# A transformer block on one core: other load, evaluation and weight orders at both ends of the kernel

## The chip, the cores and the metric

The kernel runs on one core of one Trainium2 chip. The metric is the device time of one execution in microseconds, as the median of several runs. The core's engines are TensorE (PE, with its weight loads listed apart as PEld), VectorE (DVE), ScalarE (ACT), GpSimd (POOL) and SyncE (SP), which issues all DMAs of this kernel.

## The reference

A pre-norm block of multi-query attention, followed by a pre-norm gated feed-forward part. The sequence has 2048 tokens, the width D is 1024, there are 32 query heads of width 32 with one K and one V head, and F is 3584. All tensors are bf16.

```python
def layernorm(x):                      # no scale, no shift
    return (x - mean(x)) / sqrt(var(x) + 1e-5)

x  = A_x                               # [1, 2048, 1024]; B_x is not used
n  = layernorm(x)
q  = n @ wq                            # 32 heads of 32
k, v = n @ wk, n @ wv                  # one head of 32
p  = softmax(q k^T / sqrt(32))
h  = x + (p @ v, heads joined) @ wo
n2 = layernorm(h)
out = h + (sigmoid(n2 @ w_gate) * (n2 @ w_up)) @ w_down
```

## The kernel before, in words

**Tiles.** The tokens are 16 tiles of 128 (index t). A "half" hf is one token tile with 16 of its 32 heads, so there are 32 halves, and a "visit" is one half against one key tile kt: 512 visits. For each visit PE runs four S matmuls of 32 rows side by side (`emit_S`, L657), and ACT takes their 128 x 2048 scores through exp in two instructions of 1024 columns (L675) into a slot of bf16. There are 11 slots of their own (`Pr`) and 4 borrowed buffers (`QTb`, `hnT`, `hact`, `h_sb`) at the start. S lives in three pairs of PSUM banks, everything else that PE computes goes through two banks, `F_ps`.

**Stages of a half.** P V is done in parts of several key tiles (`mk_PV`, L737, `PARTS`, L691: 0 to 8 and 8 to 16), each part a group of matmuls with Vt; a slot comes free when its P V has run. The softmax sums are added up by DVE (`acc`, L650) and reduced by a small matmul group (`mk_SUM`). Half 0 (`RAW`) has its sums from a second set of P V groups with a matrix of ones. `finish` multiplies by the reciprocal sums into `OT`. The two halves of a token tile then give the output projection (`mk_OP`, L825), the second norm and the transposed `hnT` by DMA.

**Feed-forward.** Pass t (`mk_GU`, L927) has 7 groups of 512 columns of F. Gate and up are 8 matmuls each with `hnT` as the stationary and a weight slab as the moving operand (512 columns), so the result has tokens on the partitions. ACT makes tanh of the gate (L944), DVE joins it with up into `act_s` (L953), and a DMA transpose brings it to `hact` (L957). Down (`mk_D`, L977) is 4 groups of 28 matmuls of 256 columns with `wd_sb`. Slabs of gate and up stream in from memory for each pass (`load_next`, L888); the last two groups of a pass are kept for the next one, which runs in the opposite direction. w_down is loaded once (`load_wd`, L515), as the space of the first norms' tiles comes free, and a D group waits for all of it.

**Start.** x and the weights of Q, K, V are loaded in a written order (L293 to L315). The first norm's statistics are two DVE instructions per tile, an aggregate and two casts; the reciprocal root is made on POOL by an add and two powers (`stats`, L332, L357 to L363). Tiles 0 to 3 are transposed by PE (`mk_xT`), the later ones by DMA (`x_by_dma`, L391). K and V follow in `mk_KV`, Q for the first two tiles in `mk_Qc` (128 columns), for the others in `mk_Q`, which stores Q to memory to be read back by pairs of tiles. PSUM evictions go to ACT or DVE, whichever the planner has free first (`evac`, L263).

**What sets the order.** A planner in Python (`Plan`, L43) runs when the program is built. It holds estimated times for every instruction and a model of the DMA queue (`step`, L98; `LATE`, L45), picks for PE what to run next, and writes one fixed list per engine. On the chip each engine runs its list in order and waits on semaphores. PE's choices: an S as soon as its inputs are known and ACT has less than `run` of work queued; otherwise the group in hand, or the first ready class of `PRIOS` (L420), chosen by `qf`. `TUNE` (L19) holds the settings, and `few`, `pv_few`, `sum_few`, `hmin`, `h0`, `d_off` are thresholds in these choices.

Of the kernel before, what the change touches and what calls it, by code (L numbers as in the profile page):

```python
# [12 lines left out]
P = 128  # L13
# [5 lines left out]
TUNE = dict(pace0=280, rate0=300, swait=100, parts=2, raw=1, rl=0, nd=4, pc=16, rate=300, pace=250, xd=4, qf=2,  # L19
            dall=1, wo_late=1, nkn=1, few=0, rmin=600, hmin=3, h0=200, h1=350, hf=1.0, run=700, sum_few=0,  # L20
            pv_few=3, d_off=0, d_a=1, d_b=1, eb=0, eq=100)
# [19 lines left out]
class Plan:  # L41
# [3 lines left out]
    LATE = {"sl": 400.0, "rd": 300.0, "rb": 300.0, "hT": 400.0, "xt": 400.0, "ha": 400.0}  # L45
# [52 lines left out]
    def step(self, limit):  # L98
        best = None
        for e in self.ENG:  # L100
            h = self.heap[e]
            if h:
                s = min(self.start_of(o) for o in h)
                if best is None or s < best[0]:
                    best = (s, e)
        if best is None or (limit is not None and best[0] > limit):
            return False
        s, e = best
        h = self.heap[e]
        o = min((o for o in h if self.start_of(o) <= s + 1e-9), key=lambda o: (o.prio, o.seq))  # L110
        h.remove(o)
        if o.pace and self.pace_free > s:
            s2 = self.pace_free
            prev = [a for a in self.lists["act"][-6:] if a.end <= s2]
            if prev:
                o.deps.append(prev[-1])
            s = s2
        self.free[e] = s + o.occ
        o.start = s
        if o.nbytes:  # L120
            if o.pace:
                self.pace_free = s + o.nbytes / TUNE["pace0" if self.fast(s) else "pace"]
            go = max(s + 1500.0, self.dma_free)
            self.dma_free = go + o.nbytes / TUNE["rate0" if self.fast(s) else "rate"]
            o.end = self.dma_free + 750.0 + self.LATE.get(o.key.rstrip("0123456789_"), 0.0)
        else:
            o.end = s + o.lat
        o.pos = len(self.lists[e])
        self.lists[e].append(o)
        for u in o.users:  # L130
            u.ready = max(u.ready, o.end)
            u.missing -= 1
            if u.missing == 0:
                self.heap[u.eng].append(u)
        o.users = []
        return True
# [21 lines left out]
def bass_sequential_preLN__grouped_kv_mqa__glu_gated_glu__prompt_kernel(  # L158
# [31 lines left out]
    with ExitStack() as es:  # L190
# [113 lines left out]
        load_x(2)  # L304
        load_x(3)
        load_wq(0)
        for t in range(4, 6):
            load_x(t)
        load_wq(1)
        for t in range(6, 12):  # L310
            load_x(t)
        load_wq(2)
        for t in range(12, NT):
            load_x(t)
        load_wq(3)  # L315
# [16 lines left out]
        def stats(ph, tiles, srcs, deps, prio):  # L332
# [8 lines left out]
            for t, src, dp in zip(tiles, srcs, deps):  # L341
                s = n_st[0] % 8
                n_st[0] += 1
                a = pl.op("dve", lambda s=s, src=src: DVE.bn_stats(st[:, s, 0, :], src[:, 0:512]), dp, prio=prio,  # L344
                          occ=600, lat=756, order=[st_user.get(s)])
                b = pl.op("dve", lambda s=s, src=src: DVE.bn_stats(st[:, s, 1, :], src[:, 512:1024]), dp, prio=prio,  # L346
                          occ=600, lat=756, order=[st_user.get(s)])
                c = pl.op("dve", lambda s=s, t=t: DVE.bn_aggr(mv[:, ph, t, :], st[:, s, :, :]), [a, b], prio=prio - 1,
                          occ=110, lat=284)
                st_user[s] = c  # L350
                ag.append(c)
# [4 lines left out]
                      occ=90, lat=250)  # L356
            f = pl.op("pool", lambda: POOL.tensor_scalar(  # L357
# [11 lines left out]
        for tiles in ([0], [1], [2, 3], [4, 5], [6, 7], [8, 9], [10, 11], [12, 13], [14, 15]):  # L369
            r = stats(0, tiles, [x_sb(t) for t in tiles], [[x_ld[t]] for t in tiles], 3)  # L370
            for t in tiles:
                sv1[t] = r
        xnorm = {}
        xcent = {}
        for t in range(NT):
# [32 lines left out]
        make_norm1(0, [])  # L408
        make_norm1(1, [])
# [9 lines left out]
        head = ["xT", "KV", "Q0", "PV", "SUM", "OP", "hT"]  # L419
# [237 lines left out]
        def emit_S(v):  # L657
# [26 lines left out]
            if kt + 1 in PARTS:  # L684
                if kt == NT - 1 and hf not in RAW:
                    queues["SUM"].append(mk_SUM(hf))
                queues["PV"].append(mk_PV(hf, PARTS.index(kt + 1) - 1))
                if hf in RAW:
                    queues["PV"].append(mk_PV(hf, PARTS.index(kt + 1) - 1, True))

        PARTS = [(), (), (0, 8, 16), (0, 5, 10, 16), (0, 6, 11, 16), (0, 4, 8, 12, 16)][TUNE["parts"]]  # L691
# [6 lines left out]
        def in_row(few):  # L698
            return v_done[0] >= NV or pl.pe_mode == "row" or len(free_slots) <= few
# [22 lines left out]
        def finish(hf):  # L722

            if hf not in rb_ld or (hf, len(PARTS) - 2) not in oun_ev:
                return
# [6 lines left out]
                [oun_ev[(hf, len(PARTS) - 2)], op_last.get(c - 1)] + rb_ld[hf], prio=0, occ=600, lat=690)  # L732
# [4 lines left out]
        def mk_PV(hf, part, sums=False):  # L737

            kts = range(PARTS[part], PARTS[part + 1])
            final = part == len(PARTS) - 2  # L740

            def atoms(b):
                return [(mm(F_ps[DH * j:DH * (j + 1), b, :], ones[:, :] if sums else Vt[:, kt, :], slot_of[(hf, kt)][:, j * 512:(j + 1) * 512],
                            kt == kts[0], kt == kts[-1], tile_position=(0, DH * j)), 512, "col" if j == 3 else "col-", [],
# [30 lines left out]

            def first():
                return [exp_of[(hf, kt, i)] for kt in kts for i in range(2)] + [c_one if sums else v_ev.get(kt) for kt in kts]
# [149 lines left out]
        def mk_GU(t, i):  # L927

            gr = group_of(t, i)
            ho = hact[:, :].rearrange("p (a f b) -> p a f b", a=2, b=P)[:, t % 2, 4 * gr:4 * gr + 4, :]  # L930

            def atoms(w):
                def a(b):
                    us, ops = slab_at[(t, i, w)]
                    return [(mm(F_ps[:, b, :], hnT[:, dt, t % 2, :], us[dt // 4][:, dt % 4, :], dt == 0, dt == DT - 1),
                             512, "dense", [ops[dt // 2]] if dt % 2 == 0 else []) for dt in range(DT)]
# [12 lines left out]
            def after_u(b, last):  # L949
                k = n_act[0]  # L950
                n_act[0] += 1
                so = act_s[:, k % NST, :]
                e = pl.op("dve", lambda: DVE.scalar_tensor_tensor(  # L953
                    out=so, in0=tnh[:, :], scalar=1.0, in1=F_ps[:, b, :],
                    op0=ALU.add, op1=ALU.mult), [last, box["a"], act_dma.get(k - NST)], prio=0, **t_dve(512))
                box["e"] = e
                act_dma[k] = dma(lambda: SP.dma_start_transpose(ho, so), f"ha{t % 2}_{gr}", P * 1024, [e] + gu_deps(t),  # L957
                                 prio=0, occ=700.0)
                for f in range(4):
                    hact_ev[(t, 4 * gr + f)] = act_dma[k]  # L960
# [276 lines left out]
```

## Time and profile before

| | us |
|---|---|
| median of 4 runs | 1112.63 (1111.87 to 1114.09) |
| the profiled execution's own time | 1110.98 |
| its span, first to last instruction | 1109.2 |
| PE busy, share of the span | 1077.6 (97%) |
| ACT busy | 1009.4 (91%) |
| DVE busy | 836.2 (75%) |
| POOL busy | 65.7 (6%) |
| the 1008 exps into `Pr` (L675) | 945.1 |
| the 112 tanh (L944) | 70.5 |

In the profile a row of a group names the line, the engine, what is written and read, the shape and the count, then the busy time and the mean of one instruction. Nearly all matmuls have line 423, where the helper `mm` makes them, and are told apart by their operands: `S_ps<-QTb,kT` is S, `F_ps<-ring,hnT` or `F_ps<-Pr,hnT` is gate or up (with the slab in the ring or in former slots), `F_ps<-zone,hact` is down, `F_ps<-Pr,Vt` is P V, `F_ps<-wo_sb,OT` the output projection, `F_ps<-acc,sel` the sums, `F_ps<-zone` Q, K and V. In the rows by time, the first number is the start, the second the length of the merged stretch, and square brackets hold the idle time before it and the instruction that ended it. Matmuls overlap, so the busy time of PE does not say how much work it could still take; the distance from the start of one to the start of the next does.

### The profile page before, as it was taken

The numbers are of one execution on the slowest core, as the hardware profiler recorded it, in microseconds if no ns is written. First come the engines' busy times: TensorE is split into PE (matmuls) and PEld (weight loads), VectorE is DVE, ScalarE is ACT, GpSimd is POOL, SyncE is SP. The second block draws the span as 40 slices with busy tenths as digits, with TensorE's granted clock in tenths as the row PEclk, the third lists the DMA queues.
The fourth block names the chain that finished last, engine by engine and source line by source line (L and its number), as shares of the span: only waits on it lengthen the run. The fifth ranks groups of instructions, "written<-read, shape, count | busy, mean of one in ns | idle before, by whom it ended". The sixth has DMA issues, their size and how long they took to land.

```text
span 1109.2 us, 23778 instructions
## 1 busy us (share of the span) xinstructions
PE 1077.6 (97%) x9608; PEld 487.6 (44%) x9608; DVE 836.2 (75%) x1039; ACT 1009.4 (91%) x1160; POOL 65.7 (6%) x97
## 2 busy tenths in 40 slices
PE   5899997999999999999999999999999999999998
PEld 4533332444444444444444444444444444444456
DVE  8867978687777878787877878787877878787311
ACT  4899999999999999999999999999999999999010
POOL 4200100010010101010010101010010101010000
PEclk9999998999999999999999999999999999999999
DMA  9884499788959597887968597878958586988995
GB/s 262 177 264 145 108 297 261 208 225 195 268 152 239 158 256 176 226 217 200 254 161 239 150 265 177 225 217 174 282 159 239 160 242 167 232 216 196 277 294 135
DMA packets 305470, 235.56 MB, mean 212 GB/s; under 512 B 108496, under 2 KB 291792, under 8 KB 305360
## 3 DMA queue, kind: packets, MB, share of 16 engines
q1 hardware_dynamic: 305360, 234.03, 80.3%
q8 instruction: 76, 1.25, 0.5%
q14 instruction: 34, 0.28, 0.1%
HBM read 203.82 MB, written 8.12 MB: 191 GB/s over the span
## 4 chain that ended last, share of the span: by engine, by line
PE 70%; ACT 18%; DVE 6%; DMA 3%; issue 2%; SPq 1%; POOL 0%; POOLq 0%; DVEq 0%; ACTq 0%
PE F_ps L423 59%; ACT Pr L675 16%; PE S_ps L423 11%; DVE acc L650 2%; ACT tnh L944 1%; DVE st L344 1%; DVE st L346 1%; DMA rb<-r_scratch 1%; DMA ring<-in_B_w_gate_dram 1%; DMA hnT<-hn 0%; DMA Pr<-in_B_w_up_dram 0%; DMA ring<-in_B_w_up_dram 0%; DVE ring L393 0%; DVE ring L381 0%; DMA r_scratch<-r_sb 0%
## 5 line engine op out<-in xcount | busy, mean ns | idle before, releaser
L675 ACT ACTIVATE Pr<-S_ps 128x1024 bf16<-128x1024 f32 x1008 | 945.1, 1059 | 8.7 <-PE S_ps L423 8.4
L650 DVE TENSOR_TENSOR acc<-acc,Pr 128x2048 bf16<-128x2048 bf16 x430 | 525.1, 1221 | 79.0 <-ACT Pr L675 64.1
L423 PE MATMUL F_ps<-ring,hnT 128*128 128x512 bf16 x1672 | 413.4, 381 | 2.4 <-DMA ring<-in_B_w_up_dram 0.8
L423 PE MATMUL F_ps<-zone,hact 128*128 128x256 bf16 x1792 | 230.6, 275 | 1.0 <-DMA hact<-act_s 0.6
L423 PEld LDWEIGHTS F_ps<-ring,hnT 128*128 128x128 bf16 x1672 | 142.7, 97 | 191.2 <-issue 60.5
L423 PE MATMUL S_ps<-QTb,kT 32*128 32x512 bf16 x2048 | 202.8, 386 | 8.4 <-ACT Pr L675 7.1
L423 PEld LDWEIGHTS F_ps<-zone,hact 128*128 128x128 bf16 x1792 | 163.8, 98 | 68.1 <-issue 34.3
L423 PEld LDWEIGHTS S_ps<-QTb,kT 32*128 32x128 bf16 x2048 | 51.4, 91 | 193.1 <-ACT Pr L675 143.3
L423 PE MATMUL F_ps<-Pr,Vt 128*32 128x512 bf16 x2016 | 135.3, 382 | 0.9 <-ACT Pr L675 0.6
L944 ACT ACTIVATE tnh<-F_ps 128x512 f32<-128x512 f32 x112 | 70.5, 629 | 58.2 <-PE F_ps L423 58.2
L953 DVE SCALAR_TENSOR_TENSOR act_s<-tnh,F_ps 128x512 bf16<-128x512 f32 x112 | 76.6, 684 | 40.0 <-PE F_ps L423 38.2
L423 PE MATMUL F_ps<-zone 128*128 128x512 bf16 (+3 forms) x584 | 76.8, 279 | 2.7 <-DVE Vt L273 1.6
L423 PEld LDWEIGHTS F_ps<-Pr,Vt 128*32 128x32 bf16 x2016 | 43.9, 95 | 62.4 <-issue 27.2
L423 PE MATMUL F_ps<-wo_sb,OT 128*128 128x512 bf16 x256 | 64.0, 381 | 1.8 <-DVE OT L729 0.9
L357 POOL TENSOR_SCALAR zb<-mvb 128x1 bf16<-128x1 bf16 (+1 forms) x25 | 7.0, 282 | 977.4 <-DVE mvb L353 977.2
L770 DVE TENSOR_TENSOR oun<-F_ps,oun 128x512 f32<-128x512 f32 x32 | 22.1, 692 | 43.3 <-PE F_ps L423 43.3
L423 PEld LDWEIGHTS F_ps<-zone 128*128 128x128 bf16 x584 | 39.7, 99 | 31.8 <-issue 11.1
L990 DVE SCALAR_TENSOR_TENSOR h_sb<-F_ps,h_sb 128x256 bf16<-128x256 f32 x64 | 26.8, 419 | 33.6 <-PE F_ps L423 33.6
L712 DVE RECIPROCAL r_sb<-F_ps 128x64 f32<-128x64 f32 x31 | 17.3, 558 | 28.3 <-PE F_ps L423 28.2
L729 DVE TENSOR_TENSOR OT<-oun,rb 128x512 bf16<-128x512 f32 x32 | 22.0, 688 | 20.9 <-DMA rb<-r_scratch 20.9
L423 PEld LDWEIGHTS F_ps<-wo_sb,OT 128*128 128x128 bf16 x256 | 21.0, 97 | 35.7 <-issue 11.6
L650 DVE TENSOR_TENSOR acc<-Pr 128x2048 bf16<-128x2048 bf16 x31 | 36.0, 1163 | 0.0
(70 smaller groups left out, 319.5 us busy)
## 6 DMA issues: line engine op xcount, KB each, us to landing
ring<-in_B_w_gate_dram SPq DMA_DIRECT2D x308, 256.0 KB, 4.1
ring<-in_B_w_up_dram SPq DMA_DIRECT2D x304, 256.0 KB, 4.2
rb<-r_scratch SPq DMA_DIRECT2D x124, 64.0 KB, 2.9
zone<-in_B_w_down_dram SPq DMA_DIRECT2D x14, 512.0 KB, 5.0
Pr<-in_B_w_up_dram SPq DMA_DIRECT2D x24, 256.0 KB, 5.2
Pr<-in_B_w_gate_dram SPq DMA_DIRECT2D x20, 256.0 KB, 4.8
ring<-in_A_x_dram SPq DMA_DIRECT2D x16, 256.0 KB, 6.0
h_sb<-in_A_x_dram SPq DMA_DIRECT2D x16, 256.0 KB, 2.7
```

Source lines behind the costliest of these rows:

```text
L344: a = pl.op("dve", lambda s=s, src=src: DVE.bn_stats(st[:, s, 0, :], src[:, 0:512]), dp, prio=prio, occ=600, lat=756, order=[st_user.get(s)])
L346: b = pl.op("dve", lambda s=s, src=src: DVE.bn_stats(st[:, s, 1, :], src[:, 512:1024]), dp, prio=prio, occ=600, lat=756, order=[st_user.ge ...
L357: f = pl.op("pool", lambda: POOL.tensor_scalar(out=zb[:, ph, tk], in0=mvb[:, ph, tk, 1], scalar1=LN_EPS_BF16, scalar2=None, op0=ALU.add), ...
L423: return lambda: PE.matmul(o, lhsT=l, rhs=r, start=start, stop=stop, **kw)
L650: add_op[(hf, kt)] = pl.op("dve", lambda: DVE.tensor_tensor(out=a, in0=in0, in1=slot, op=ALU.add), dp, prio=6, **t_dve(2048, 1.92))
L675: exps[u] = pl.op("act", lambda i=i, pb=pb: ACT.activation(out=slot[:, i * 1024:(i + 1) * 1024].rearrange("p (a b) -> p a b", a=2), in_=S_ ...
L712: rc = pl.op("dve", lambda: DVE.reciprocal(r_sb[:, :], F_ps[:, b, 0:64]), [last, rd_ld.get(hf - 1)], prio=0, occ=64 * 8 / 0.96 + 20, lat=6 ...
L729: ot_ev[hf] = pl.op("dve", lambda: DVE.tensor_tensor(out=OT[:, 4 * hh:4 * hh + 4, :], in0=o.rearrange("p (a b) -> p a b", a=4), in1=r.rear ...
L770: oun_ev[(hf, part)] = pl.op("dve", lambda: DVE.tensor_tensor(out=o, in0=F_ps[:, b, :], in1=o, op=ALU.add), [last, oun_ev[(hf, part - 1)]] ...
L944: box["a"] = pl.op("act", lambda: ACT.activation(out=tnh[:, :], in_=F_ps[:, b, :], func=ACTF.Tanh, scale=0.5), [last, box.get("e")], prio= ...
L953: e = pl.op("dve", lambda: DVE.scalar_tensor_tensor(out=so, in0=tnh[:, :], scalar=1.0, in1=F_ps[:, b, :], op0=ALU.add, op1=ALU.mult), [las ...
L990: e = pl.op("dve", lambda: DVE.scalar_tensor_tensor(out=h_sb[:, t % NHB, sl], in0=F_ps[:, b, 0:DW], scalar=0.5, in1=h_sb[:, t % NHB, sl], ...
```

## The change

- The loads of wq's four quarters stand ahead of most x tiles: after x0, x1, wk and wv the order is x2, wq0, x3, wq1, x4, wq2, wq3, then the other x tiles.
- For tiles 0 and 1, the add and the reciprocal of the first norm run on DVE; only one power stays on POOL. The statistics of the first tiles are ordered after the centring of the tile before (`after`).
- P V parts of half 0 are key tiles 0 to 5, 5 to 10 and 10 to 16, those of half 1 are 0 to 6, 6 to 11 and 11 to 16. The later halves keep two parts.
- `qf` puts Q ahead of gate/up and down in PE's choice.
- In passes 0, 14 and 15 gate and up take the weight slab as the stationary and `hnT` as the moving operand: 32 matmuls of 128 columns in place of 8 of 512. The result has F on the partitions, so DVE writes `hact` itself, and there is no DMA transpose.
- The planner's DMA model and thresholds have other values, so the order of all lists shifts somewhat. In the lists, the order from the 97th S to the 480th has the same counts of each kind of work between S as before. After the last S there are 800 matmuls of 128 columns for gate and up (before: 184 of 512), 289 for down (288), and as before one P V part, one sum and 16 for the output projection. Ahead of the first S stand 8 transposes, 40 matmuls of 128 columns and 8 of 32 (before: 32, 48 with 7 of 256, and 16). The DMA transposes of `act_s` go from 112 to 91.

```diff
-TUNE = dict(pace0=280, rate0=300, swait=100, parts=2, raw=1, rl=0, nd=4, pc=16, rate=300, pace=250, xd=4, qf=2,
-            dall=1, wo_late=1, nkn=1, few=0, rmin=600, hmin=3, h0=200, h1=350, hf=1.0, run=700, sum_few=0,
-            pv_few=3, d_off=0, d_a=1, d_b=1, eb=0, eq=100)
+TUNE = dict(late=100, ws0=1, ws1=2, parts0=3, parts1=4, lord=2, h_ord=0, ho=0, ho2=3, pvl1=0, pvl2=0, col_ok=0,
+            pace0=310, swait=100, parts=2, raw=1, rl=0, nd=4, pc=16, rate=315, pace=310, xd=4, qf=1, dall=1,
+            wo_late=1, nkn=1, few=1, rmin=600, hmin=1, h0=0, h1=350, hf=1.0, run=700, sum_few=1, pv_few=4,
+            d_off=2, d_a=1, d_b=1, eb=0, eq=100)
...
-    LATE = {"sl": 400.0, "rd": 300.0, "rb": 300.0, "hT": 400.0, "xt": 400.0, "ha": 400.0}
+    LATE = {"sl": 465.0, "hT": -90.0, "xt": 100.0, "wd": -100.0, "xr": -300.0, "rb": -250.0, "ql": -500.0, "qs": -200.0,
+            "o": -500.0, "wo": 700.0, "x": -435.0}
+
+    SLOW = {"rb": 1.9, "ha": 2.5, "ql": 1.6, "wq": 1.1}
...
-        load_x(2)
-        load_x(3)
-        load_wq(0)
-        for t in range(4, 6):
-            load_x(t)
-        load_wq(1)
-        for t in range(6, 12):
-            load_x(t)
-        load_wq(2)
-        for t in range(12, NT):
-            load_x(t)
-        load_wq(3)
+        for c in ["xxqxxqxxxxxxqxxxxq", "qxqxxqxqxxxxxxxxxx", "xqxqxqqxxxxxxxxxxx", "xqxqxqxqxxxxxxxxxx", "xxqxqxqxqxxxxxxxxx"][TUNE["lord"]]:
+            if c == "x":
+                load_x(len(x_ld))
+            else:
+                load_wq(len(wq_ld))
...
+            if not ph and t0 < 2:
+
+                f = pl.op("dve", lambda: DVE.tensor_scalar(
+                    out=zb[:, ph, tk], in0=mvb[:, ph, tk, 1], scalar1=LN_EPS_BF16, scalar2=None, op0=ALU.add),
+                    [d], prio=prio - 1, occ=90, lat=250)
+                g = pl.op("pool", lambda: POOL.tensor_tensor(
+                    out=dsb[:, ph, tk], in0=zb[:, ph, tk], in1=half[:, 0:k], op=ALU.pow), [f, c0], prio=0,
+                    **slow(460 + 180 * k, 0))
+                h = pl.op("dve", lambda: DVE.reciprocal(rstd[:, ph, tk], dsb[:, ph, tk]), [g], prio=prio - 1, occ=90, lat=250)
+                return e, h
...
+            after = ((), ())
+            if tiles[0] in (1, 2):
+
+                p = tiles[0] - 1
+                after = (([sv1[p][0], xcent[p]], [xnorm[p]]), ([], [xnorm[p]]), ([xnorm[p]], ()), ([sv1[p][0], xcent[p]], ()))[TUNE["ho"] if p == 0 else TUNE["ho2"]]
...
+        def parts_of(hf):
+            return PARTS[TUNE["parts" if hf > 1 else "parts0" if hf == 0 else "parts1"]]
...
+            held_w = t < TUNE["ws0"] or t >= NT - TUNE["ws1"]
...
+                    if held_w:
+                        return [(mm(F_ps[:, b, k * P:(k + 1) * P], us[dt // 4][:, dt % 4, k * P:(k + 1) * P], hnT[:, dt, t % 2, :],
+                                    dt == 0, dt == DT - 1), P, "dense", [ops[dt // 2]] if k == 0 and dt % 2 == 0 else [])
+                                for k in range(4) for dt in range(DT)]
...
+                if held_w:
+                    e = pl.op("dve", lambda: DVE.scalar_tensor_tensor(
+                        out=ho, in0=tnh[:, :].rearrange("p (f b) -> p f b", b=P), scalar=1.0,
+                        in1=F_ps[:, b, :].rearrange("p (f b) -> p f b", b=P),
+                        op0=ALU.add, op1=ALU.mult), [last, box["a"]] + gu_deps(t), prio=0, **t_dve(512))
+                    done = e
```

## The prediction

> **What bounds the kernel now.** I read the page's slices first, to find where the engines are not full, then ScalarE's (ACT) and TensorE's (PE) instructions in order of time, then sums over chosen stretches. The slices:
>
> ```profile
> PE   5899997999999999999999999999999999999998
> ACT  4899999999999999999999999999999999999010
> PEclk9999998999999999999999999999999999999999
> ```
>
> One slice is 27.7 us. ACT is full from the third slice to the 37th and nearly empty in the last three; PE is short in slices 1, 2 and 7, and in the 7th its clock drops too. So there are three stages: a head, a long stretch in which ACT sets the pace, and a tail in which ACT has nothing and PE alone works. Sums by stretch (length, busy PE, PE weight load, DVE, ACT, POOL; clock; DMA share; GB/s):
>
> ```profile
> 50.00:90.00 40.00, 39.81 (x364) 15.55 (x362) 22.21 (x28) 35.50 (x40) 0.00 (x0) 1.00 0.76 245
> ...
> 185.00:198.00 13.00, 8.79 (x90) 4.51 (x86) 7.96 (x10) 10.89 (x13) 0.31 (x1) 0.74 0.50 131
> ...
> 380.00:1026.50 646.50, 646.50 (x5781) 285.69 (x5778) 514.98 (x591) 646.13 (x737) 30.37 (x30) 1.00 0.80 210
> 1026.50:1109.20 82.70, 76.22 (x539) 46.69 (x537) 19.16 (x34) 6.57 (x11) 1.35 (x3) 1.00 0.92 235
> ```
>
> From 380 to 1026.5 us ACT idles 0.4 us of 646.5: nothing that leaves its work alone can shorten this part. ACT's idle time sits in the head, and its exps are released by PE's S matmuls (square brackets: idle before, and who ended it):
>
> ```profile
> 19.25 2.85 ACT L675 ACTIVATE Pr<-S_ps 128x1024 bf16<-128x1024 f32 x3 [0.72 <-PE S_ps L423]
> ...
> 54.13 11.14 ACT L675 ACTIVATE Pr<-S_ps 128x1024 bf16<-128x1024 f32 x12 [2.28 <-PE S_ps L423]
> 84.07 0.60 ACT L272 ACTIVATE hact<-F_ps 128x512 bf16<-128x512 f32 x1 [0.42 <-PE F_ps L423]
> 86.47 4.69 ACT L675 ACTIVATE Pr<-S_ps 128x1024 bf16<-128x1024 f32 x5 [1.80 <-PE S_ps L423]
> ...
> 195.06 4.72 ACT L675 ACTIVATE Pr<-S_ps 128x1024 bf16<-128x1024 f32 x5 [2.11 <-PE S_ps L423]
> ```
>
> The first exp is at 19.25, the last ends at 1026.4. In between ACT is idle 9.5 us by the stretches (0.6 to 36 us, 0.7 to 50, 4.5 to 90, 0.2 to 140, 0.5 to 185, 2.1 to 198, 0.6 to 380, 0.4 after), so it works 997.7 us. **The ledger** is: first exp + ACT's work + its idle time, then the tail.
>
> PE in the tail, and one stretch of the head that prices a 128-column matmul:
>
> ```profile
> 25.16 2.51 PEld L423 LDWEIGHTS F_ps<-zone 128*128 128x128 bf16 x43 [0.23 <-issue]
> ...
> 1034.89 3.62 PE L423 MATMUL F_ps<-ring,hnT 128*128 128x512 bf16 x16
> 1038.34 1.67 PE L423 MATMUL F_ps<-Pr,hnT 128*128 128x512 bf16 x7
> ...
> 1060.87 3.22 PE L423 MATMUL F_ps<-zone,hact 128*128 128x256 bf16 x28
> 1063.93 2.75 PE L423 MATMUL F_ps<-Pr,hnT 128*128 128x512 bf16 x12
> ...
> 1096.71 9.78 PE L423 MATMUL F_ps<-zone,hact 128*128 128x256 bf16 x88 [0.59 <-DMA hact<-act_s]
> ```
>
> Start to start, a 512-column gate/up matmul takes 3.45/16 = 0.2156 us, a 256-column down matmul 3.06/28 = 0.1093, a 128-column one 2.51/43 = 0.0584. PE's last work before the last exps is an S at 1023.9; its tail runs from 1024.23 to 1106.49: 82.3 us. By the order of instructions it holds 184 gate/up (39.7 us), 288 down (31.5), 16 output-projection (3.45), one P V part (1.84) and one sum (0.42): 76.9. The other 5.4 are waits and drains: 3.7 are bracketed, 1.4 of these on DMAs (hnT 0.21, late slabs 0.33 and 0.28, the transposed hact 0.59). After PE come 2.7 us of output.
>
> **What the Trainium skill says.** "TensorE: Matmul & The Clock Gate", section "Back-to-back issue gap", gives N/2.4 + 2.5 ns for the isolated matmul (56 ns at N=128), but about 81 ns for a stream of weight load and matmul at N=128. The trace has 58.4 in such a stream, so I take 58.4; 56 and 81 are my bounds. The same page, "What's actually happening", says that PE's clock halves after about 3.4 us of little activity. The trace agrees: at 191.3 us, after waits, 14 down matmuls take 3.15 us (0.225 each, not 0.109). "GPSIMD Engine Reference", 3.1, has two software dispatch hops for each POOL instruction; here a 128x1 pow is 0.53 us (1.06 for two), a DVE cast of 128x2 0.17.
>
> **The change, part by part.**
>
> *First norms.* Tile 0 waited on POOL: behind four wk copies (to 6.36), then zb, pow and reciprocal pow, each interleaved with tile 1's; its normalisation started at 9.74 and the transposes at 10.27. After: add and reciprocal on DVE (no row for this size; 0.1 to 0.56, the 128x64 reciprocal; I take 0.17), one pow after only one wk copy. Worked through DVE's new order: statistics from 3.41, aggregate 4.7, zb ends 5.4, pow 5.45 to 6.0, reciprocal 6.3, then one x2 statistics half (0.6) that stands ahead of the normalisation and waits for x2 (issued 2.73, 3.8 us to land: 6.5). Normalise 7.1, transpose 7.65: 2.6 us earlier. The three wk copies now end near 7.1, before K needs them at 9.5.
>
> *Order to the first S.* Before, both tiles' transposes and K stood ahead of it; now 8 transposes, K, V and 32 Q matmuls of tile 0. From 7.65: 1.07 to the eviction, 0.69 on DVE (ACT took 1.02), K at 9.5, K/V to 10.75 at the cold clock, Q to 13.4 (half cold), 0.8 to S, 0.45 to exp: **first exp 14.7, 4.5 us earlier.** Second exp pair: tile 1's chain is now behind tile 0's on DVE: S at 17.75, exp 18.2, ACT idle 1.3. DVE carries four evictions (0.61) where it had two, and the kT ones; summing its new order puts tiles 2-3's kT at 24.3, the fifth S at 24.8 (28.09 before), ACT idle again 0.7. So 1.6 us of new idle time net of the old.
>
> *wq ahead of x.* wq1 follows 2.1 MB, not 2.6 (landed 12.7): near 11, needed at 12.2. On SP's queue x4 onward moves behind up to 1 MB, about 3 us at 350 GB/s; x5, due by 13.7 before, comes by 16 and DVE takes it at 18. Hidden by about 2 us; without that cover it costs what is late. The DMA transposes behind them wait for DVE anyway.
>
> *Small P V parts.* Idle at 54.13 and 86.47 is PE in a block of 32 + 32 P V matmuls that must free slots, after waiting for the eighth tile. Parts of 5 and 6 tiles start earlier. Between S 24 and 32 PE had 16.7 us of work (56 Q 12.1, P V 2.0, S 2.6) against ACT's 14.7 for 16 exps; the new order has at most 14.3 in any eight S. I take 4.3 of the 4.5 us as gone. Three more evictions, 2.1 us, lie on DVE, which is idle 17.8 of 40 us there.
>
> *Q ahead of gate/up, pass 0 held.* At 185 to 198 PE starved: pass 0's hidden tiles were transposed by DMA, and the last w_down loads (issued to 185.1, 5.0 us each) came at 190, so PE idled, cooled, and D ran at half rate: ACT's 2.11. Now Q ends by S 64, 9 of 14 w_down loads stand ahead of pass 0's later slabs (6 before), hact needs no DMA, and S 65 to 96 has 54.5 us of PE work against ACT's 62.3. That 7.8 us also covers pass 0's own excess: 448 x 0.0584 - 112 x 0.2156 = 2.0. I take 2.1 gone, and 0.9 of the small DMA-caused gaps from 140 to 380.
>
> *Ledger.* 14.7 + 997.3 (one tanh less, 0.48, ahead of the last exp) + idle 9.5 - 7.3 + 1.6 = 3.8: the last exp ends at 1015.8, **10.6 earlier.**
>
> *Tail, weights held in passes 14 and 15.* PE now has 800 matmuls of 128 columns after the last S, which is 200 of 512: 16 more than before, work that the shorter head left undone (it is not free: 3.4 us), and the dearer form (2.8 more). 46.7 + 289 x 0.1093 + 3.45 + 1.84 + 0.42 = 84.0. Waits 5.4 - 1.4 = 4.0, as no transposed hact is waited for, and 10 transposes leave the saturated DMA (1.1 share, 288 GB/s from 1040 to 1090) while 2 MB more slabs come: about even, with PE slower. Tail 88.0, **5.7 longer.** At 56 or 81 ns it is 3.8 or 23.8 longer. Next in the way is PE's own work.
>
> *Sum.* -10.6 + 5.7 = -4.9. The profiled execution took 1110.98 us (span 1109.2), 0.15% below the median of the runs, 1112.63; I apply the difference to the median: **1107.7 us.**
>
> **Rivals.**
>
> *A, more comes back.* The tail's waits mostly go (2.3 more) and DVE's lag costs nothing (2.0): 1103.4. For: the tail's largest wait, 0.93 on OT, has filler. Against: P V and the sum still end one chain.
>
> *B, the idle time only moves.* PE's order is fixed: a D group that meets a late w_down load holds all S behind it, or the x2 wait on DVE delays tile 0. If only 2.4 of the 7.3 us go, -5.7 + 5.7 = 0: 1112.6. For: five w_down loads still stand at the end of pass 0. Against: PE has work ahead of them.
>
> *C, slower.* Held-weight matmuls run at the skill's streaming 81 ns, as each must load its own weights: 800 x 0.0226 = 18.1 more in the tail: 1125.8. It decides from 0.0584 + 4.9/800 = 64.5 ns. Against: 43 in a row at 58.4.
>
> That the change does not take place is excluded by the order of instructions.
>
> **How the numbers follow.** Forecast 0.56, A 0.20, B 0.13, C 0.11. Measurement tells about 0.2% from no change: below 1110.4 is faster, above 1114.9 slower. Forecast, A and a little of B: faster 0.79; the rest of B and an edge of the others: same 0.11; C and B's worst: slower 0.10. C and half of B are left out of the range, 1101.5 to 1112.8.
>
> **What would show it.** Right: first exp near 14.7; no ACT gap over 1 us from 50 to 200; clock whole there; last exp near 1016; tail near 88; 128-column gate/up matmuls 58 ns apart. Wrong: long ACT idle at the second or fifth S; D stalled near S 90; over 64 ns per held matmul; slab waits in the tail.

## The result, and the profile after

The changed kernel takes 1109.43 us, the median of 34 runs (1106.85 to 1113.43); the kernel before takes 1112.64 beside it (53 runs, 1110.27 to 1115.61). The ratio is 0.9971, 95% interval 0.9965 to 0.9976: 3.2 us faster, where the forecast was 4.9. The profiled execution took 1110.42 (span 1108.6), 1.0 above its median, and that of before 1110.98 (span 1109.2), 1.7 below its own. So the two traces differ by only 0.6 us, and what follows reads stages, not spans.

The slices of the changed kernel (27.7 us each):

```profile
PE   6899999999999999999999999999999999999999
ACT  4999999999999999999999999999999999998010
PEclk9999999999999999999999999999999999999999
```

PE's seventh slice is full now (9, before 7), ACT's second too (9, before 8), and the clock is whole, where it had an 8 in the seventh slice. Sums by stretch (length, busy PE, PE weight load, DVE, ACT, POOL; clock; DMA share; GB/s), the last two cut at the new end of the exps:

```profile
50.00:90.00 40.00, 39.08 (x402) 15.26 (x403) 31.83 (x43) 39.69 (x45) 1.47 (x2) 1.00 0.85 269
185.00:198.00 13.00, 11.67 (x107) 5.39 (x104) 11.53 (x13) 13.00 (x16) 0.00 (x0) 1.00 0.60 189
380.00:1023.50 643.50, 639.82 (x5814) 285.67 (x5811) 509.00 (x582) 639.40 (x727) 30.35 (x30) 1.00 0.79 207
1023.50:1108.60 85.10, 80.71 (x1146) 73.65 (x1143) 19.98 (x35) 7.24 (x13) 1.34 (x3) 1.00 0.75 232
```

ACT's idle in 50 to 90 us fell from 4.50 to 0.31, and in 185 to 198 from 2.11 to nothing. But from 380 us on ACT idles 4.1 us, where it had idled 0.4. ACT in order of time shows where (some of its longer pieces of idle time, in square brackets):

```profile
15.54 1.94 ACT L690 ACTIVATE Pr<-S_ps 128x1024 bf16<-128x1024 f32 x2 [0.59 <-PE S_ps L438]
...
312.31 1.94 ACT L690 ACTIVATE Pr<-S_ps 128x1024 bf16<-128x1024 f32 x2 [0.92 <-PE S_ps L438]
...
565.35 1.94 ACT L690 ACTIVATE Pr<-S_ps 128x1024 bf16<-128x1024 f32 x2 [0.92 <-PE S_ps L438]
...
691.54 1.94 ACT L690 ACTIVATE Pr<-S_ps 128x1024 bf16<-128x1024 f32 x2 [0.83 <-PE S_ps L438]
...
1003.94 4.71 ACT L690 ACTIVATE Pr<-S_ps 128x1024 bf16<-128x1024 f32 x5 [1.01 <-PE S_ps L438]
```

Each of the late ones is an S that PE issued late, and PE's own waits name what held it. Who waited for whom, PE and its weight load, 198 to 1005 us (total us, times, longest); in the kernel before no DMA is in this list:

```profile
PE F_ps L438 <- DMA ring<-in_B_w_up_dram: 4.9, 10, 1.0
...
PEld F_ps L438 <- DMA ring<-in_B_w_up_dram: 13.6, 20, 1.4
```

So slabs of the up weights arrive late. PE in the tail:

```profile
1032.13 3.74 PE L438 MATMUL F_ps<-hnT,ring 128*128 128x128 bf16 x64
1035.70 1.11 PE L438 MATMUL F_ps<-hnT,Pr 128*128 128x128 bf16 x17
1038.10 1.89 PE L438 MATMUL F_ps<-wo_sb,OT 128*128 128x512 bf16 x8 [1.29 <-DVE OT L748]
...
1093.56 12.39 PE L438 MATMUL F_ps<-zone,hact 128*128 128x256 bf16 x112
```

64 matmuls of 128 columns take 3.57 us from start to start (1032.13 to 1035.70), 55.8 ns each, each with a stationary of its own. The only long wait is 1.29 on OT, and nothing waits for a DMA.

To set runs side by side I added the gaps between ACT's instructions in order of time, from one numbered exp to another (of 1024; two make a visit), and took the time from the end of PE's last S to its last matmul as the tail. All in us; the ratio is to the kernel before on the same chip, and the last column is the median time from the first issue of the seventh group's up slab to its first use (the weight load of the group's first up matmul), passes 2 to 12; a dash is a time that was not read. Single runs apart, the kernel before had medians between 1111.25 and 1112.64 beside these, so the ratio decides, and ratio x 1112.6 puts a run on the scale of the expectations.

| kernel | ratio (95%) | first exp | idle to exp 65 | 65 to 185 | 185 to 1024 | last exp ends | tail | issue to use |
|---|---|---|---|---|---|---|---|---|
| before | 1 | 19.25 | 5.8 | 2.8 | 0.9 | 1026.4 | 82.2 | 15.2 |
| changed | 0.9971 (0.9965-0.9976) | 15.54 | 3.4 | 0 | 6.5 | 1023.6 | 84.4 | 4.6 |
| pace 250 | 0.9975 (0.9965-0.9985) | 15.12 | 3.1 | 0 | 5.5 | 1022.1 | 85.8 | 5.1 |
| tail of 512 columns | 1.0003 (0.9992-1.0015) | 15.23 | 2.9 | 0 | 3.9 | 1020.3 | 87.5 | 4.4 |
| x first | 1.0019 (1.0008-1.0030) | 16.07 | 4.6 | 0.8 | 7.3 | 1027.8 | 83.7 | 4.5 |
| two P V parts | 1.0050 (1.0032-1.0069) | 15.48 | 8.9 | 0.7 | 7.1 | 1031.7 | 86.4 | 6.1 |
| resident weights | 0.9933 (0.9919-0.9947) | 15.55 | 3.2 | 0 | 3.4 | 1019.1 | 84.7 | - |
| D one group later | 1.0009 (0.9998-1.0020) | 15.41 | 2.9 | 0 | 7.2 | 1022.8 | 85.9 | 6.4 |
| GpSimd reciprocals | 1.0099 (1.0077-1.0120) | 16.43 | 1.1 | 0.7 | 6.9 | 1020.1 | 104.4 | - |
| Q late | single run | 15.42 | 2.9 | 0.6 | 7.2 | 1020.2 | 110.6 | - |
| store late | 0.9950 (0.9938-0.9962) | 15.53 | 3.2 | 0 | 2.9 | 1018.9 | 83.3 | 5.3 |
| hnT late | 0.9959 (0.9946-0.9972) | 14.85 | 3.0 | 0 | 3.2 | 1019.1 | 83.7 | 6.5 |
| both late | 0.9960 (0.9948-0.9973) | 14.91 | 3.2 | 0 | 3.4 | 1018.9 | 83.4 | 7.0 |
| no order of norms | single run | 17.73 | 1.0 | 0 | 9.2 | 1022.8 | 103.5 | - |

### The profile page after: what moved, and what is told of

Its sections match the earlier page's. It is cut to its first block, busy times and chain, and to the rows that moved or that the text cites. A ratio compares the mean times of both kernels' runs of the same rounds, so it can differ in the third digit from the quotient of the medians.

```text
span 1108.6 us, 25728 instructions
## 1 busy us (share of the span) xinstructions
PE 1079.3 (97%) x10616; PEld 531.6 (48%) x10616; DVE 842.7 (76%) x1051; ACT 1007.5 (91%) x1155; POOL 65.2 (6%) x93
## 3 DMA queue, kind: packets, MB, share of 16 engines
q8 instruction: 84, 1.38, 0.5%
HBM read 203.82 MB, written 8.12 MB: 191 GB/s over the span
## 4 chain that ended last, share of the span: by engine, by line
PE 57%; ACT 31%; DMA 5%; DVE 4%; issue 2%; SPq 1%; POOL 0%; DVEq 0%
PE F_ps L438 48%; ACT Pr L690 29%; PE S_ps L438 9%; DMA ring<-in_B_w_up_dram 2%; ACT tnh L972 2%; DVE acc L665 1%; DMA r_scratch<-r_sb 1%; DMA rb<-r_scratch 0%; DMA zone<-ring 0%; DMA ring<-in_A_x_dram 0%; DVE st L342 0%; DVE ring L398 0%; DVE st L344 0%; DVE ring L386 0%; SPq L929 0%
## 5 line engine op out<-in xcount | busy, mean ns | idle before, releaser
L665 DVE TENSOR_TENSOR acc<-acc,Pr 128x2048 bf16<-128x2048 bf16 x429 | 523.9, 1221 | 78.1 <-ACT Pr L690 62.3
L438 PE MATMUL F_ps<-ring,hnT 128*128 128x512 bf16 x1456 | 361.8, 381 | 5.2 <-DMA ring<-in_B_w_up_dram 4.9
L438 PEld LDWEIGHTS F_ps<-ring,hnT 128*128 128x128 bf16 x1456 | 123.2, 97 | 172.4 <-issue 53.3
L438 PEld LDWEIGHTS F_ps<-zone,hact 128*128 128x128 bf16 x1792 | 163.1, 98 | 63.4 <-issue 32.7
L988 DVE SCALAR_TENSOR_TENSOR act_s<-tnh,F_ps 128x512 bf16<-128x512 f32 x91 | 62.2, 684 | 23.5 <-PE F_ps L438 21.3
L438 PE MATMUL F_ps<-hnT,ring 128*128 128x128 bf16 x912 | 61.0, 219 | 1.4 <-DMA ring<-in_B_w_gate_dram 1.0
L438 PEld LDWEIGHTS F_ps<-hnT,ring 128*128 128x128 bf16 x912 | 52.4, 98 | 9.9 <-issue 7.6
L438 PEld LDWEIGHTS F_ps<-zone 128*128 128x128 bf16 x584 | 40.5, 100 | 34.2 <-issue 11.1
```

The lines of the kernel that those rows point to most:

```text
L438: return lambda: PE.matmul(o, lhsT=l, rhs=r, start=start, stop=stop, **kw)
L665: add_op[(hf, kt)] = pl.op("dve", lambda: DVE.tensor_tensor(out=a, in0=in0, in1=slot, op=ALU.add), dp, prio=6, **t_dve(2048, 1.92))
L988: e = pl.op("dve", lambda: DVE.scalar_tensor_tensor(out=so, in0=tnh[:, :], scalar=1.0, in1=F_ps[:, b, :], op0=ALU.add, op1=ALU.mult), [las ...
```

## The experiments

**First round: is it the pace of the transfers, and what is each part worth?** My first theory was that SyncE's list and its pacing make slabs late; its rival, that PE's own order does.

Pace 250: `TUNE: pace=310` becomes `pace=250`.

> The changed kernel with the pace of its transfers at 250 bytes per ns, as the kernel before had it, instead of 310: TensorE's order stays the same but for one spot of three matmuls in the tail, only the order and the spacing of SyncE's issues in the middle differ. Theory 1 (the 7.6 us of the lead that are lost between 198 and 1022 us go to gate/up slabs that land late, because SyncE's list puts stores and transposes ahead of them): the waits of PE for ring<-in_B_w_up_dram (18.5 us of idle in front of PE's F_ps groups in the middle) change clearly with the list. If this pace restores the old spacing, ACT's idle in 198:1000 falls from 5.5 to 1-2 us, the last exp ends 3 to 5 us earlier and the time is 1104.5 to 1106.5. Theory 2 (the loss comes from PE's own order, as D matmuls or P V parts that stand ahead of a score): nothing moves, 1109.4 +- 0.6, ACT's idle in the middle 5 to 6 us. A time above 1111 would say that the list matters but that 310 is the better pace of the two.

Measured: ratio 0.9975, ACT's idle in the middle 5.5 us, slab waits of 3.4 (PE) and 12.8 (weight load) in place of 4.9 and 13.6. The pace is not the cause; the waits survive another spacing.

Tail of 512 columns: `ws1=2` becomes `ws1=0`.

> The changed kernel with the weights-held form of gate/up only in pass 0, so the last two passes stream 512 columns again (200 matmuls of 512 in the tail for 800 of 128, one D matmul fewer) and their products go through a DMA transpose. All up to the last exp is as in the changed kernel. Theory 1: the held form costs 800 x 0.0557 = 44.6 us in the tail and the other 200 x 0.2156 = 43.1, so 1.5 us of work are saved here, and PE waits again for the transposed products, 1 to 4 us as in the tail of the kernel before: 1109 to 1112, the tail 84 to 87 us, last exp unchanged. Rival (the held form saves the tail nothing, its waits were hidden by D matmuls): 1107.5 to 1108.5, tail near 83.

Measured: ratio 1.0003, 0.32% above the changed kernel's, 3.6 us; tail 87.5. PE in that tail, where products go through a DMA transpose again:

```profile
1060.36 0.61 PE L438 MATMUL F_ps<-zone,hact 128*128 128x256 bf16 x4 [3.04 <-DMA hact<-act_s]
...
1095.85 9.78 PE L438 MATMUL F_ps<-zone,hact 128*128 128x256 bf16 x88 [0.64 <-DMA hact<-act_s]
```

Two waits of 3.7 us in all for transposed products: the held form costs 1.5 us of work and saves these. The expectation's first theory holds in its mechanism; the time (1.0003 x 1112.6 is 1113.0) and the tail lie somewhat above its ranges. This run has the changed kernel's lists up to its last passes, yet lost 3.9 us in the middle where the changed kernel's profiled execution lost 6.5. So what late slabs cost differs between executions with the same lists, and one profiled execution does not tell it to better than some 2.6 us.

x first: `lord=2` becomes `lord=0`, the old order of loads.

> The changed kernel with the old order of loads (wq's quarters after x tiles 3, 5, 11 and 15), all else as changed; TensorE's order of the tail and SyncE's list of the middle are the same. Theory 1 (Q's weights bind the first exp once the norms are short): first exp 2 to 3 us later than 15.5, near 18, and the lead that is lost is carried to the end of the first half or further: 1110 to 1112. Rival (the first dozen exps are bound by the norms and the later tiles, so that by exp 21 the order of loads no longer shows): first exp later by as much, but the time 1109.4 +- 0.7, because at exp 21 both are alike.

Measured: 1.0019, 0.48% or 5.3 us worse than the changed kernel, of which 2.5 are there by exp 185 (199.28 against 196.78). The first exp moved by only 0.5, not by 2 to 3. The fifth moved, from 20.75 to 25.69: ACT waits 2.31 and 1.38 us for PE's Q and K between them. So the order of loads pays, but not where I expected it, and both statements on the first exp were wrong.

Two P V parts: `parts0=3, parts1=4` become `2, 2`.

> The changed kernel with the old P V parts (0, 8, 16) in halves 0 and 1 too. Theory 1 (the small parts take away the gaps of ACT at about 54 and 84 to 86 us): one or both gaps come back within 50 to 95 us, 2 to 4.5 us of ACT idle there against 0.3, and the time is 1111.5 to 1114. Rival (the gaps went with the earlier Q, or the lead gained there is lost again to late slabs in the middle whatever its size): the gaps come back or not, but the time stays within 1108.5 to 1110.5.

Measured: 1.0050. ACT in order of time shows that both gaps are back:

```profile
53.31 3.77 ACT L690 ACTIVATE Pr<-S_ps 128x1024 bf16<-128x1024 f32 x4 [1.80 <-PE S_ps L438]
58.32 7.44 ACT L690 ACTIVATE Pr<-S_ps 128x1024 bf16<-128x1024 f32 x8 [1.24 <-PE S_ps L438]
87.07 0.60 ACT L277 ACTIVATE hact<-F_ps 128x512 bf16<-128x512 f32 x1 [2.98 <-PE F_ps L438]
```

The idle time to exp 65 is 8.9, 5.5 more. The theory on the small parts holds; the rest of the loss (8.8 us in all) lies behind, in an order that the planner has changed as well, with one stop of 2.88 us at 621.

**Second round: which slab, and why.** Set against the times of the groups, PE's waits for slabs fall in the seventh, the last group of a pass. In pass 8 the seven groups start, from the first one's start, at 0, 4.3, 15.4, 26.5, 35.1, 51.3 and 57.9 us before, and the next pass at 62.3; after, at 0, 11.1, 22.2, 30.8, 46.9, 53.5 and 58.0, and the next at 63.4. It is the same sequence of gaps, turned by one group. (Counts of work between the S are the same as before, as said with the change; they do not show which group falls where.) Before, the close pair behind the seventh was the first and second group, and their slabs are resident. After, it is the sixth and seventh, and the seventh needs new slabs, in slots that come free when the fifth is done. What SyncE does at that point of the changed kernel, in order of time (start, length of issue):

```profile
675.06 0.36 SPq L1032 DMA_DIRECT2D out_dram<-h_sb  x1
676.51 1.12 SPq L929 DMA_DIRECT2D ring<-in_B_w_gate_dram  x2
678.06 0.35 SPq L844 DMA_DIRECT2D h_sb<-in_A_x_dram  x1
678.46 0.94 SPq L929 DMA_DIRECT2D ring<-in_B_w_gate_dram  x2
679.45 2.57 SPq L875 DMA_TRANSPOSE hnT<-hn  x1
682.06 1.26 SPq L991 DMA_TRANSPOSE hact<-act_s  x1
683.37 1.61 SPq L929 DMA_DIRECT2D ring<-in_B_w_up_dram  x3
685.09 0.48 SPq L733 DMA_DIRECT2D r_scratch<-r_sb  x1
685.61 0.59 SPq L929 DMA_DIRECT2D ring<-in_B_w_up_dram  x1
```

SyncE issued nothing from 668.5 to 675.06: it stood at the store, which waits for the pass's last D (DVE adds that one to `h_sb` at 674.62, for 0.42 us). Over the middle these stores are the second largest of SyncE's waits (total us, times, longest; the row names the DVE cast that ends next to that addition):

```profile
SPq L929 <- PE F_ps L438: 148.4, 55, 6.7
SPq L1032 <- DVE mvr L353: 83.8, 13, 6.8
```

The row of the kernel before:

```profile
SPq L997 <- DVE mvr L355: 48.7, 13, 4.0
```

The fifth group's last matmul starts at 677.8, so its slot is free shortly after; the up slab is issued from 683.37 to 685.61, behind a store, a load and two transposes, and PE, which comes to the group's up matmuls at 687.4 (first weight load), waits in front of the last three of the eight:

```profile
688.65 1.08 PE L438 MATMUL F_ps<-ring,hnT 128*128 128x512 bf16 x3
690.34 0.82 PE L438 MATMUL F_ps<-ring,hnT 128*128 128x512 bf16 x3 [0.61 <-DMA ring<-in_B_w_up_dram]
691.10 0.40 PE L438 MATMUL S_ps<-QTb,kT 32*128 32x512 bf16 x4
```

The S behind these six matmuls is the one that ACT waits 0.83 us for, at 691.54. That is theory 3: PE's turned order together with what stands ahead of the slab on SyncE.

Resident weights: in passes 3 to 13, group 7 reads the slabs of group 6.

```
-us, ops = slab_at[(t, i, w)]
+us, ops = slab_at[(t, i - (i == NGR - 1 and 2 < t < 14), w)]
```

What the group waits for has the same new index. The seventh group's own slabs are still loaded, but the group leaves them out and computes with the sixth group's weights, which are in memory by then. So the output is not the block's, and the kernel serves only to time the wait.

> The changed kernel, in which the seventh (last) gate/up group of passes 3 to 13 reads the resident weights of the sixth group in place of its own, which are still loaded as before; the lists of all engines and of SyncE are the same, only the wait of PE for that group's slabs is gone (and the product is that of other weights). New theory (3): the changed order of PE is the old one turned by one group. Before, two groups that need no new slab (the first two of a pass) followed each other closely; now the last one of a pass, which needs new ones, starts 11 us after the group whose slot it reuses ended its turn, and its up slab is issued only 4 to 5 us ahead of its first use (before, the least of all slabs was 11 us). Theory 3: ACT's idle between exps 185 and 1024 falls from 6.5 to under 1.5 us, the last exp comes at 1016 to 1018, the time is 1103.5 to 1106. Rival (the slab waits in the trace are covered by scores that are ready anyway; the loss is D or P V work ahead of scores): idle stays over 4 us, 1108.5 to 1110.

Measured: ratio 0.9933, against 0.9971, intervals apart; idle in the middle 3.4; last exp at 1019.1. With every list unchanged, taking away this one wait gives 0.38%, 4.2 us. Theory 3 stands, its rival is out. The idle time fell less than to 1.5, and the last exp is not at 1016 to 1018: 1.7 us of the idle time lie ahead of exp 321, before the alias acts.

D one group later: `d_off=2` becomes `1`.

> The changed kernel with d_off=1 for 2: the head is the same up to about exp 170, then PE takes the D matmuls of a pass one group later, and the gaps between gate/up groups change so that no group follows the last but one by less than 21 us on the scale of PE's list (16.8 in the changed kernel, 20.1 in the one before). Tail: 789 gate/up matmuls of 128 (800) and 308 D (289), 19 x 0.109 - 11 x 0.056 = 1.5 us more. Theory 3: no wait of PE for a slab in the middle, idle between exps 185 and 1024 under 2 us (6.5), last exp near 1017.5, with the tail 1105 to 1107. Rival (slabs are late for want of DMA bandwidth whatever the order): idle stays 4 to 7 us, 1110.5 to 1112.

Measured: 1.0009; the waits for the up slab stayed (6.4 and 14.0 us), idle 7.2. By its numbers this run went the rival's way, want of DMA bandwidth; the third round decides against that rival for the changed kernel's order. My number was the wrong one: the gap in PE's list grew, but the slab's last quarter was issued as little as 1.0 us ahead of the group's first up matmul (1.25 in the changed kernel, 6.6 at the least for any slab before). The gap between groups only bounds when the slab can be issued. The tail, 1.5 us longer, came as worked out; the whole loss against the changed kernel is 0.38%, 4.2 us, and what lies beyond the tail is not explained.

GpSimd reciprocals: `if not ph and t0 < 2:` becomes `if False:`.

> The changed kernel with the reciprocals of the first two norms on GpSimd again. The planner then gives another order everywhere after the first scores, and leaves 96 more gate/up matmuls of 128, 27 of 512 and 47 D after the last score: 5.4 + 5.8 + 5.1 = 16 us more tail, so 1115 to 1126 in all. What is to be read is the head: theory 1: first transpose near 10 us (8.03 in the changed kernel, 10.27 before), first exp near 17.5. Rival (the 2.2 us came from the order of DVE's queue or from the loads): first transpose within 0.4 of 8.0.

Measured: 1.0099, with a tail of 104.4, the planner's doing. The first transpose is at 8.12, not at 10: the rival is right. DVE and POOL around tile 0's norm in that run, then DVE in the changed kernel:

```profile
6.88 0.55 POOL L371 TENSOR_TENSOR rstd<-dsb,cst 128x1 f32<-128x1 bf16 x1
...
7.54 0.52 DVE L393 TENSOR_SCALAR zone<-ring,rstd 128x1024 bf16<-128x1024 bf16 x1 [0.20 <-POOL rstd L371]
```

```profile
6.65 0.15 DVE L363 RECIPROCAL rstd<-dsb 128x1 f32<-128x1 bf16 x1
6.89 0.69 DVE L344 BATCH_NORM_STATS2 st<-ring 128x6 f32<-128x512 bf16 x1
7.50 0.47 DVE L393 TENSOR_SCALAR zone<-ring,rstd 128x1024 bf16<-128x1024 bf16 x1
```

The reciprocal is ready 0.6 us earlier on DVE, but the half of statistics that stands ahead of the normalisation eats that: 0.04 us remain.

Q late: `qf=1` becomes `2`.

> The changed kernel with gate/up ahead of the remaining Q projections again. The order differs from the 60th score group on, and the planner leaves some 24 us more work after the last score (96 x 0.056 + 48 x 0.216 + 75 x 0.109): 1120 to 1135. To be read: theory 1: an idle piece of ACT of 1 to 3 us between 180 and 205, with PE's clock cold around it, as before at 195. Rival (the gap went with the held form of pass 0 or the small P V parts): no gap there, clock whole.

Measured: 1133.0 beside 1111.6. The clock is whole in every slice, and ACT has no gap over 0.4 us from 150 to 203, then 0.95 at 203 and 1.32 at 236. Neither theory's picture came out. With the rest of the change in place the cold stretch at 195 does not return; which part removed it is not settled, as the held form of pass 0 was not tried alone.

**Third round: the list of SyncE, with PE's order kept.** An extra delay in the planner moves SyncE's entries; PE's, ACT's and POOL's orders are as in the changed kernel. (On DVE 18 of 1051 instructions change places with the late store, 2 with both moves, none with the late hnT.)

```
-        s = max(self.free[o.eng], o.ready)
+        s = max(self.free[o.eng], o.ready + o.delay)
```

with a delay of 8000 ns for output stores or of 3000 ns for transposes of hnT, each in the middle passes, or both, in all passes.

> The changed kernel with the output stores of passes 3 to 13 put 8 us later in SyncE's list; the order on TensorE, ScalarE and all else is the same. In the changed kernel the pass's last store holds SyncE 6.8 us a pass (it waits for the last D), with the gate slab, the transpose of hnT and the up slab of the seventh group queued behind it. Theory 3 with the store alone as the cause: the up slab is issued 5 us earlier, the slab waits go, 1105 to 1106.5. Theory 3 with both (after the store, the transposes of hnT and hact still stand ahead of the up slab, and hn is ready only at 553 of the 551 at which the slot comes free): the up slab is issued 0 to 2 us earlier, some of the waits stay, 1107 to 1109. Rival (the slot itself comes free too late): 1109 to 1110, issue to first use under 5 us as before.

> The changed kernel with the transposes of hnT of passes 3 to 13 put 3 us later in SyncE's list, behind the up slab of the seventh group; the store stays ahead. Order elsewhere the same. Theory 3 with both: the up slab is issued 1.5 to 2.5 us earlier than in the changed kernel, 1106.5 to 1108.5; with the store alone as the cause: 1109 to 1110. A loss would be hnT late for the next pass's first group (it lands 5 us after its issue and is used some 12 us after it): over 1111.

> Both moves, in all passes: stores 8 us and transposes of hnT 3 us later in SyncE's list, order elsewhere the same. Theory 3: the up slab of the seventh group is issued when its slot comes free, about 5 us earlier, first use 9 us after issue; no slab waits of PE in the middle, ACT's idle between exps 185 and 1024 under 3 us (6.5), 1104 to 1105.5, as with the resident weights read in its place (1105.2) or better. Rival (slabs late for want of bandwidth whatever the list): over 1108.

Measured: 0.9950, 0.9959 and 0.9960, idle in the middle 2.9, 3.2 and 3.4, last exp at 1018.9 to 1019.1. PE's waits for the up slab fall from 4.9 us (13.6 in front of its weight loads) to 1.5 (4.2), 0.7 (4.0) and none. In the profiled executions PE's last matmul is 5.4 to 5.9 us ahead of the changed kernel's; the ratios give 2.3, 1.3 and 1.2 us.

The store alone brings the issue forward by only 0.7 us in the median, not by 5, and some waits stay: this is the mild form of theory 3, in which other entries stand ahead of the slab as well. Its time fits that too (0.9950 x 1112.6 is 1107.1). The hnT move does it as well, in its expected range (1108.1). With both moves the waits went, as theory 3 said, but the time (1108.2), the idle time (3.4) and the 7.0 us from issue to use missed their expectations (1104 to 1105.5, under 3, and 9). The rival of want of bandwidth is out: from 198 to 1000 us the DMA share is 0.81 and the rate 209 GB/s, as good as the changed kernel's 0.81 and 208, and no slab is late.

With both moves SyncE issues the slab in one piece, in pass 8 some 2.5 us after the end of the fifth group's last matmul (5.2 in the changed kernel), behind the rest of the gate slab and one transpose:

```profile
674.07 2.52 SPq L938 DMA_DIRECT2D ring<-in_B_w_gate_dram  x4
676.96 1.20 SPq L1000 DMA_TRANSPOSE hact<-act_s  x1
678.22 2.22 SPq L938 DMA_DIRECT2D ring<-in_B_w_up_dram  x4
680.49 1.40 SPq L884 DMA_TRANSPOSE hnT<-hn  x1
```

and PE's list of waits from 198 to 1022 us has no DMA left:

```profile
PE F_ps L447 <- DVE oun L795: 2.0, 5, 0.6
PE F_ps L447 <- DVE h_sb L1034: 0.7, 2, 0.5
```

What is late next is DVE's eviction of P V, 0.2 us before. Of the three intervals only that of the store lies clear of the changed kernel's, so "0.2% faster than the changed kernel" (2.3 us) is shown for that one alone. The interval of the resident weights (0.9919 to 0.9947) does not meet that of both moves (0.9948 to 0.9973), although both kernels end their exps alike (1019.1 and 1018.9) and the profiled execution of the latter is the shorter (1104.75 against 1106.27 us). Each has only 5 or 6 runs. That late slabs cost time is shown; how much of the 4.2 us belongs to them is not settled.

No order of norms: the lists `after` of the first two tiles stay empty, the reciprocals stay on DVE.

```
-            if tiles[0] in (1, 2):
+            if False:
```

> The changed kernel with the reciprocals on VectorE, but without the order that holds tile 1's statistics behind tile 0's norm: VectorE takes both tiles' statistics first, as before the change, and TensorE transposes both tiles ahead of K. All later order differs as well, with about 16 us more work after the last score (1115 to 1130 in all), so only the head is read. Theory 4 (after the run with GpSimd's reciprocals had its first transpose at 8.11, the gain of 2.2 us in the head is from the order of VectorE's queue, not from where the reciprocal runs): first transpose 9.3 to 10.3, first exp 17 to 19. Rival (either of the two alone is enough): first transpose within 0.5 of 8.0.

Measured: first transpose 9.61, first exp 17.73: theory 4. DVE's queue has other tiles' work between the steps of tile 0 again, and tile 0's reciprocal has its turn at 8.42, where the changed kernel had it at 6.65:

```profile
8.42 0.16 DVE L363 RECIPROCAL rstd<-dsb 128x1 f32<-128x1 bf16 x1
8.49 0.68 DVE L344 BATCH_NORM_STATS2 st<-ring 128x6 f32<-128x512 bf16 x1
9.08 0.47 DVE L393 TENSOR_SCALAR zone<-ring,rstd 128x1024 bf16<-128x1024 bf16 x1
```

Of the 2.2 us by which the first transpose came earlier, 1.6 come back without the order and 0.1 without the reciprocals. Both of these kernels start their exps later than the changed one, and yet reach exp 65 earlier (80.6 and 79.6 us against 82.0): putting tile 0 first delays the tiles behind it. Their later orders differ too, so that this is a reading and not a proof.

## Why the prediction was right in its sum, and where it was wrong

The direction is right and the size within 1.7 us, but two terms were off, by 7.8 and 3.6 us, and offset each other in part. That the sum came out so near is luck.

- *First norms and order to the first S:* transpose 8.03 (7.65), first exp 15.54 (14.7), second pair 18.64 (18.2), fifth S 25.80 (24.8). The mechanism holds, each step 0.4 to 1.0 later than forecast. The cause that I named first, the reciprocals on DVE, is worth almost nothing once the order of DVE's queue is there (0.1 of 2.2); without that order 1.6 are lost.
- *wq ahead of x:* "hidden by about 2 us" was only the cost of moving x back. The move pays 0.48% when all else is changed.
- *Small P V parts:* 4.3 of 4.5 us were to go, 4.2 went, and the gaps return without the parts. Right.
- *Q ahead, pass 0 held:* ACT's 2.11 us at 195 are gone and the clock is whole, as forecast. Which of the two did it is open. The "0.9 of the small DMA-caused gaps from 140 to 380" is wrong: from 198 to 380 ACT idles 2.4 us (182.00 - 179.60), where it idled 0.6.
- *Ledger:* this is the step that failed. From the first exp to the last, ACT's idle time is 9.9, not 3.8: 3.4 to exp 65, none to 185, 6.5 after. The first exp is 0.8 later than forecast, and ACT's work is 1023.6 - 15.5 - 9.9 = 998.2 (forecast 997.3); with these the last exp is 7.8 later. By exp 185 the changed kernel was 10.4 us ahead (196.78 against 207.19), as forecast for the end, but 7.6 of the lead were lost by the last exp (1022.56 against 1025.34). Of these, 5.6 are idle time (6.5 against 0.9). The other 2.0 lie in the work: the same exps and tanh take 819.3 us in place of 817.3, and 818.0 to 818.3 in the runs with resident weights, the late store and both moves; why is open. I had read "ACT idles 0.4 us of 646.5" as a property of the stage. It belonged to one order of PE and SyncE in which each new slab was issued at least 10.9 us ahead of its first use; nothing in the sum checked that the new order keeps this. It does not, and rival B, which looked for stops in the head, did not name it either.
- *Tail:* 84.4, not 88.0. The 128-column matmul takes 55.8 ns, not 58.4 (44.6 us for 800, 2.1 less). The 58.4 was a row's length divided by its count, and that row of 43 weight loads holds a pause from 26.57 to 26.77 us; nearly all others in it come 55 to 58 ns apart, so the trace of before had the right price already. (The 0.225 for cold down matmuls has a like flaw: from start to start it is 0.21.) The waits are 84.4 - 81.9 = 2.5, not 4.0 (81.9 is the forecast's sum of work with 44.6 for 46.7). By the forecast's own prices the held form is 46.7 - 43.1 = 3.6 dearer, not 2.8, though its total has it right. In the balance I had the sign wrong: the held form is 3.6 us better than the 512-column form, since it does without the transposed products.
- *Rivals:* C needed more than 64.5 ns for a held matmul, and 55.8 rules it out. A wanted 2.3 us less waiting in the tail; 1.5 came.

So the ledger's term was 7.8 us too good at the last exp, and the tail 3.6 too bad. In the profiled execution that leaves 0.6 us of the 4.9; the median, 3.2, lies higher, which fits the smaller loss (3.9) that the one other profiled execution with these lists in the middle shows; two executions do not prove it.

In pass 8 of the changed kernel four other entries stand between the moment when a slot is free and the slab's issue. That PE's order is turned by one group is seen, but not why: one gate/up group fewer is done by exp 185 (8 tanh against 9), and no run here isolates what delayed it.

## What to carry to other kernels

When a planner writes the order, a knob changes every list behind it: compare, for each streamed buffer, the time from issue to first use in the old and the new order, before holding a stage to be unchanged. A transfer that PE needs soon must not stand in an in-order issue queue behind a store that waits for a late result; where a slot is reused shortly before its next use, the entries between are worth reading one by one. A gain ahead of a stage that runs without slack shows at the end only as far as the slack of that stage's own feeds allows.

## What the runs showed of the hardware that was not expected

Matmuls of 128 columns with a new stationary each run at 55.8 ns apart over 64 in a row (changed kernel, 1032.13 to 1035.70), and those of 512 at 215.6 over 16 (kernel before, 1034.89 to 1038.34). "TensorE: Matmul & The Clock Gate" of the Trainium skill, "Back-to-back issue gap", gives 56 and 216 for an isolated matmul, and 81 and 131 for a sustained stream; here the stream has the isolated figures, and the measurement decides. A reciprocal of 128x1 on DVE took 0.15 us (changed kernel), and a power of the same size on POOL 0.55 (GpSimd reciprocals).
